# Weight blocks in halves on two DMA queues, and the second tile's statistics behind the first tile's normalising, at the head of a fused attention and FFN kernel

## Chip, cores, metric

One core of one Trainium2 chip. The metric is the device time of one execution in microseconds (us), slowest core (here the only one). The profile's span is some 1.7 to 3.5 us shorter than the time of the same run.

## The reference

```python
x  = A_x                                   # [1, 2048, 1024] bf16
xn = layernorm(x)                          # no gain, no bias
# A: 32-head linear attention
q, k, v = split(xn @ wqkv)                 # wqkv [1024, 3072]
phi = lambda t: where(t > 0, t + 1, exp(t)) + 1e-6
kv, z = phi(k).T @ v, sum(phi(k))          # per head, over all 2048 rows
s = (phi(q) @ kv / (phi(q) @ z + 1e-6)) @ wo
# B: SwiGLU
g = silu((silu(xn @ w_gate) * (xn @ w_up)) @ w_down)     # F = 3584
out = x + s * g
```

## The kernel before

The program plans itself. Every operation is put into a graph with a modelled duration; a list scheduler orders them per engine, and that order is emitted with semaphores.

Terms: a transfer is issued on SP's queue (SyncE) or ACT's (ScalarE) and lands when its last byte is there; an evacuation copies a finished product out of TensorE's result buffer `ps`; DVE is VectorE.

The head: x comes in tiles of 128 rows, the K weights in four blocks of 512 rows by 512 columns (512 KB each). I call the blocks R01 and R11 (column half j = 1, row halves k = 0 and 1; the first product needs them) and R00 and R10 (column half j = 0).

```python
def wkv_load(w, j, k):
    ap, r = kvblock(w, KB_OF[k, j])
    c0 = 1024 * (1 + w) + j * 512
    o = dma([], [r], ap, wqkv_v[:, 4 * k:4 * k + 4, c0:c0 + 512], dsem("wkv%d%d%d" % (w, j, k)), 512 * KB)
    if (w, k) == (0, 0):
        beside.append(o)                   # issued by ScalarE: R01 and R00; R11 and R10 by SP

def ln_tile(i):
    ...
    oA = dve([s.sub(0, KB).r], [sA], lambda h: h.bn_stats(stats[:, j, 0, :], xa[:, 0:512]), 512)
    oB = dve([s.sub(KB, KB).r], [sB], lambda h: h.bn_stats(stats[:, j, 1, :], xa[:, 512:1024]), 512)
    if i == 1:
        for o, q in zip((oA, oB), first):  # statistics of tile 1 wait for these two
            o.preds.add(q)
            q.succs.append(o)
    dve([sA, sB], [mvr], lambda h: h.bn_aggr(mv[:, j, :], stats[:, j, :, :]), 60)
    if i == 0:
        o0 = act([mvr, el_r], [ver], veps[:, j, :], mv[:, j, 1:2], ACT.Sqrt, "sb", bias=epsl[:, :])
        first.append(o0)
        dve([ver], [rsr], lambda h: h.reciprocal(rstd[:, j, :], veps[:, j, :]), 60)
    ...
        for c in range(0, 1024, n):        # normalise, two halves (tiles 0 and 1)
            ...
        first.append(o0)

order: x0 | x1 | R01 | R11 | R00 | R10 | x2 | V blocks ...
then:  ln_tile(0); t_tile(0); ln_tile(1); p_piece(0, 0, 1); t_tile(1); p_piece(1, 0, 1); p_piece(0, 0, 0); ...
```

`t_tile` transposes a normalised tile on TensorE (eight 128x128 blocks) and evacuates it; for tile 1 half by ScalarE, half by VectorE. `p_piece(i, 0, j)` is the product of x tile i with the K columns j, eight matmuls, evacuated by `phi_evac`: two ScalarE instructions (Exp, Relu) and two VectorE ones.

Of the kernel before, what the change touches and what calls it, by code (L numbers as in the profile page):

```python
# [14 lines left out]
KB = 1024  # L15
# [304 lines left out]
def build_kernel(nc, A_x, A_wqkv, A_wo, B_w_gate, B_w_up, B_w_down, out, WINDOW=6, NWARM=15, NPE=2, LEAD=12.0):  # L320
# [6 lines left out]
    wqkv_v = A_wqkv.rearrange("(kt p) c -> p kt c", p=128)  # L327
# [5 lines left out]
    with ExitStack() as es:  # L333
# [20 lines left out]
        def named(*key):  # L354
            return Region([key])
# [37 lines left out]
        def balloc(fresh=False):  # L393

            if fresh and bare and (len(banks) < 3 or freed[bare[0]] < freed[banks[0]]):
                b = bare.popleft()
                is_bare.discard(b)
                return b
            return banks.popleft()
# [7 lines left out]
        def bfree(b):  # L407
            freed[b] = len(PL.ops)
            (bare if b in is_bare else banks).append(b)

        def sem(name):
            return es.enter_context(nc.semaphore(name))
# [4 lines left out]
        def dsem(name):  # L417
            if name not in semn:
                semn[name] = sem("d_" + name)
            return semn[name]  # L420
# [4 lines left out]
        def mm_cost(mms):  # L425
            return sum(max(r.shape[-1] / 2400.0 + 0.0026, 0.03) * (o.shape[0] * r.shape[0] / 16384.0)
                       for (o, _, r, _, _) in mms)

        def pe_mm(reads, writes, mms):
            return PL.op("pe", reads, writes, partial(_mm_group, mms), mm_cost(mms))  # L430
# [10 lines left out]
        def act(reads, writes, o, i, func, src="ps", **kw):  # L441
            q = PL.op("act", reads, writes, lambda h: h.activation(o, i, func, **kw),  # L442
                      nel(o) / (1000.0 if "bias" in kw or not isinstance(kw.get("scale", 1.0), float) else 1200.0)
                      + (0.055 if src == "ps" else 0.095))
            if func not in (ACT.Identity, ACT.Relu):
                PL.table(q, func)
            return q

        def dve(reads, writes, fn, n, rate=0.96):
            return PL.op("dve", reads, writes, fn, n / (rate * 1000.0) + 0.07)  # L450
# [4 lines left out]
        def dma(reads, writes, o, i, s, nbytes, cow=None, after=None):  # L455
            return PL.op("sp", reads, writes, lambda h: h.dma_start(o, i), 0.47, sem=s,  # L456
                         nbytes=nbytes * (1.45 if nbytes in (128 * KB, 896 * KB) else 1.0), cow=cow,
                         after=after)
# [33 lines left out]
        def pool(reads, writes, fn, busy=0.3):  # L492
            return PL.op("pool", reads, writes, fn, busy)
# [82 lines left out]
        for n in range(NWARM):  # L576
            b = n % 8
            m = 512 if n > 3 else 128
# [154 lines left out]
        def kvblock(w, b):  # L733
            o = KV0[w] + b * 4 * KB
            return H.at(o, 4 * KB).rearrange("p (kt n) -> p kt n", n=512), H.reg(o, 4 * KB)
# [27 lines left out]
        def wkv_load(w, j, k):  # L763
            ap, r = kvblock(w, KB_OF[k, j])
            c0 = 1024 * (1 + w) + j * 512
            o = dma([], [r], ap, wqkv_v[:, 4 * k:4 * k + 4, c0:c0 + 512], dsem("wkv%d%d%d" % (w, j, k)), 512 * KB)
            if (w, k) == (0, 0):
                beside.append(o)

        xnslot = {}  # L770
        first, beside = [], []

        def ln_tile(i):
            j = i % 4
            s = xslot[i]
            xa = s.ap()
            sA, sB, mvr, ver, rsr, nmr = (named(n, j) for n in ("sA", "sB", "mv", "ve", "rs", "nm"))
# [3 lines that stand above are left out]
                for o, q in zip((oA, oB), first):  # L781
                    o.preds.add(q)
                    q.succs.append(o)
            dve([sA, sB], [mvr], lambda h: h.bn_aggr(mv[:, j, :], stats[:, j, :, :]), 60)
            if i == 0:
                o0 = act([mvr, el_r], [ver], veps[:, j, :], mv[:, j, 1:2], ACT.Sqrt, "sb", bias=epsl[:, :])
                first.append(o0)
                dve([ver], [rsr], lambda h: h.reciprocal(rstd[:, j, :], veps[:, j, :]), 60)
            else:
                o0 = dve([mvr], [ver], lambda h: h.tensor_scalar(veps[:, j, :], mv[:, j, 1:2], EPS_LN, None, ALU.add), 60)  # L790
                pool([ver, nh_r], [rsr], lambda h: h.tensor_tensor(rstd[:, j, :], veps[:, j, :], neg_half[:, :], ALU.pow), 0.56)
            o = xn_ring.take()
            xnslot[i] = o
            oa = o.ap(FP16)
            if i < 2:
                n = 512
                for c in range(0, 1024, n):
                    p0, o0 = o0, dve([s.r, mvr, rsr], [o.sub(2 * c, 2 * n).r], lambda h, c=c: h.tensor_scalar(
                        oa[:, c:c + n], xa[:, c:c + n], mv[:, j, 0:1], rstd[:, j, :], ALU.subtract, ALU.mult), n, 2.6)
                    if c:  # L800
                        o0.after = (p0,)
                        p0.succs.append(o0)
                first.append(o0)
            else:
                dve([mvr, rsr], [nmr], lambda h: h.scalar_tensor_tensor(
                    nmean[:, j, :], mv[:, j, 0:1], -1.0, rstd[:, j, :], ALU.mult, ALU.mult), 60)
                act([s.r, nmr, rsr], [o.r], oa, xa, ACT.Identity, "sb", bias=nmean[:, j, :], scale=rstd[:, j, :])

        def xt_dest(i):
            p, j, m = i // 8, (i // 4) % 2, i % 4  # L810
            ar = X if p == 0 else P
            return ar, j, m
# [26 lines left out]
        def xt_r(i, k0=0, n=KT):  # L839
            ar, j, m = xt_dest(i)  # L840
            keys = []
            for kt in range(k0, k0 + n):
                o = j * 8 * KB + kt * 1024 + m * 256
                keys += ar.reg(o, 256).keys
            return Region(keys)

        def xt_ap(i, kt):
            ar, j, m = xt_dest(i)
            return ar.at(j * 8 * KB + kt * 1024 + m * 256, 256, FP16)
# [33 lines left out]
        def k_evac(i, j, ap, r, kind):  # L883
            if i not in pkv:
                pkv[i] = pk_ring.take()
            s = pkv[i].sub(j * 1024, 1024)
            phi_evac(ap, r, s.ap(), s.r, kind, rl_rings[0])
# [4 lines left out]
        def v_evac(i, j, ap, r):  # L892
            act([r, vx_r[i % 4]], [named("vx", i % 4, j)], v_dest(i, j), ap.rearrange("p (g n) -> p g n", n=128),
                ACT.Identity)

        def p_piece(i, w, j):
            b = balloc(True)
            n = 2 if (i, w, j) == (0, 0, 1) else 4
            for k0 in range(0, KT, n):
                ap, r = KVV[w]["R%d%d" % (k0 // 4, j)]  # L900
                pe_mm([xt_r(i, k0, n), r], [bank_r[b]],
                      [(ps[b][:, :], xt_ap(i, k), ap[:, k % 4, :], k == 0, k == KT - 1) for k in range(k0, k0 + n)])
            if w == 0:
                k_evac(i, j, ps[b][:, :], bank_r[b], "ps")
            else:
                v_evac(i, j, ps[b][:, :], bank_r[b])
            bfree(b)
# [50 lines left out]
        for n, (fn, args) in enumerate(((x_load, (0,)), (x_load, (1,)), (wkv_load, (0, 1, 0)), (wkv_load, (0, 1, 1)),  # L958
# [3 lines left out]
            k = len(PL.ops)  # L962
            fn(*args)
            for o in PL.ops[k:]:
                o.urgent = 60.0 - 2 * n
        ln_tile(0)
        t_tile(0)
        tr = [o for o in PL.ops if o.eng == "pe"][-1]
        for n in range(6):
            o = pe_mm(wz_r[:1], [bank_r[kvb[2]]], [(ps[kvb[2]][:, 0:128], wz[:, 0:128], wz[:, 0:128], True, True)])  # L970
            o.preds.add(tr)
            tr.succs.append(o)
            o.urgent = -4.0
        ln_tile(1)
        p_piece(0, 0, 1)
        t_tile(1)
        p_piece(1, 0, 1)
        p_piece(0, 0, 0)
        x_load(4)
        x_load(5)  # L980
        p_piece(1, 0, 0)
        ln_tile(2)
        p_piece(0, 1, 1)
        t_tile(2)
# [60 lines left out]
        for q, kb in enumerate(kvb):  # L1045
            n = 3 if q < 2 else 2
# [777 lines left out]
```

## Time and profile before

| | before |
|---|---|
| time, median of 3 runs | 712.3 us (711.97 to 712.69) |
| profiled run | 713.57 us, span 711.8 us |
| TensorE busy | 705.0 us of the span |
| TensorE without a matmul between 5 and 10.5 us | about 0.8 us |

TensorE is the bound and has no gap from 10.51 us to far beyond; all that the change can move is the moment at which that stretch begins. The lines that show it are in the prediction.

### The profile page before, as it was taken

Reading aid. Unit: us, or ns where it says so; the run is one execution under the profiler, and the core shown is the slowest. Engines: PE = TensorE matmul, PEld = TensorE weight load, DVE = VectorE, ACT = ScalarE, POOL = GpSimd, SP = SyncE. Lnnn points to the kernel's source line nnn. Section 1 sums busy time; section 2 is a strip of 40 time slices with the busy share of each in tenths; the row PEclk is TensorE's granted clock in tenths of the full one; section 3 lists DMA queues with packets and bytes.
Section 4 is the critical chain, followed back from the end, with each engine's and each line's share of the span. In section 5 each row is a group of like instructions: output and inputs, shape, how many; then the busy total and the mean of one; then the engine's idle time right before and its main releaser. Section 6 shows DMA issues by size and latency. Waiting matters only on the chain.

```text
span 711.8 us, 11445 instructions
## 1 busy us (share of the span) xinstructions
PE 705.0 (99%) x4181; PEld 387.3 (54%) x4181; DVE 630.9 (89%) x1534; ACT 424.7 (60%) x827; POOL 12.8 (2%) x34
## 2 busy tenths in 40 slices
PE   8999999999999999999999999999999999999997
PEld 4444445555555555556555455555555555565654
DVE  6999858989999999988958989999999999797863
ACT  5788756988679566663212257876886756531212
POOL 2111000000000000000000000000000000000000
PEclk9999999999999999999999999999999999999999
DMA  9654134345664252326499955323715241646763
GB/s 310 133 99 110 30 118 123 116 143 186 187 178 141 95 171 90 119 71 175 120 233 198 215 142 149 107 73 94 207 60 192 76 149 60 184 134 168 136 160 92
DMA packets 140872, 98.66 MB, mean 139 GB/s; under 512 B 34960, under 2 KB 137872, under 8 KB 140816
## 3 DMA queue, kind: packets, MB, share of 16 engines
q1 hardware_dynamic: 139472, 96.69, 49.8%
q10 hardware_dynamic: 1344, 1.25, 0.5%
q8 instruction: 33, 0.54, 0.3%
q14 instruction: 23, 0.19, 0.1%
HBM read 77.59 MB, written 12.71 MB: 127 GB/s over the span
## 4 chain that ended last, share of the span: by engine, by line
PE 93%; DMA 3%; DVE 3%; issue 0%; SPq 0%; ACT 0%; DVEq 0%
PE ps L309 93%; DVE W L453 1%; DMA W<-in_B_w_gate_dram 1%; DMA H<-in_A_wqkv_dram 1%; DMA TM<-TM 1%; DVE TM L453 1%; DVE X L453 0%; DVE ps L453 0%; PE ps L316 0%; DVE P L453 0%; SPq L456 0%; SPq L760 0%; ACT TM L442 0%; SPq L1621 0%; DVEq L301 0%
## 5 line engine op out<-in xcount | busy, mean ns | idle before, releaser
L309 PE MATMUL ps<-X,W 128*128 128x512 f16 (+2 forms) x1372 | 288.8, 350 | 0.0
L442 ACT ACTIVATE TM<-ps 128x512 f16<-128x512 f32 (+3 forms) x386 | 202.8, 554 | 103.9 <-PE ps L309 97.8
L309 PE MATMUL ps<-H,W 128*128 128x512 f16 (+2 forms) x1096 | 218.4, 351 | 0.1
L453 DVE TENSOR_TENSOR W<-W 128x1024 f16<-128x1024 bf16 (+5 forms) x412 | 184.6, 484 | 5.0 <-PE ps L309 2.7
L309 PEld LDWEIGHTS ps<-X,W 128*128 128x128 f16 (+1 forms) x1372 | 132.1, 98 | 103.8 <-ACT H L442 1.0
L309 PEld LDWEIGHTS ps<-H,W 128*128 128x128 f16 (+1 forms) x1096 | 105.8, 98 | 95.3 <-DVE ps L453 1.1
L453 DVE TENSOR_TENSOR ps<-ps,TM 128x256 f32<-128x256 f32 (+1 forms) x250 | 132.5, 531 | 14.4 <-PE ps L309 11.2
L442 ACT ACTIVATE ps<-ps 128x512 f32<-128x512 f32 (+1 forms) x174 | 85.8, 494 | 89.9 <-PE ps L309 89.4
L442 ACT ACTIVATE H<-ps 128x512 f16<-128x512 f32 (+1 forms) x132 | 78.4, 605 | 37.9 <-PE ps L309 37.9
L309 PE MATMUL ps<-P,W 128*128 128x256 f16 (+1 forms) x516 | 99.5, 319 | 0.0
L453 DVE TENSOR_TENSOR H<-H 128x1024 f16<-128x1024 f16 (+5 forms) x126 | 71.9, 585 | 0.6 <-ACT H L442 0.4
L442 ACT ACTIVATE TM<-TM 128x512 f16<-128x512 f32 (+1 forms) x70 | 44.0, 630 | 44.5 <-DVE TM L453 43.4
L309 PEld LDWEIGHTS ps<-P,W 128*128 128x128 f16 (+1 forms) x516 | 50.1, 98 | 29.1 <-ACT TM L442 0.8
L309 PE MATMUL ps<-W 128*128 128x256 f16 (+1 forms) x330 | 62.3, 282 | 0.4 <-DVE ps L453 0.2
L453 DVE TENSOR_TENSOR H<-H,TM 128x512 f16<-128x512 f16 (+1 forms) x120 | 48.4, 420 | 8.5 <-ACT H L442 8.3
L453 DVE TENSOR_TENSOR TM<-ps,TM 128x512 f32<-128x512 f32 (+3 forms) x63 | 41.8, 663 | 12.8 <-PE ps L309 11.9
L309 PEld LDWEIGHTS ps<-W 128*128 128x128 f16 (+1 forms) x330 | 31.3, 98 | 32.6 <-DVE ps L453 1.3
L309 PE MATMUL ps<-H,X 128*128 128x512 bf16 (+1 forms) x150 | 35.2, 379 | 0.5 <-DMA H<-in_A_wqkv_dram 0.5
L453 DVE TENSOR_TENSOR TM<-TM 128x512 bf16<-128x512 f16 (+2 forms) x73 | 29.3, 414 | 7.0 <-ACT TM L442 4.3
L309 PE MATMUL ps<-H,P 128*128 128x512 bf16 (+1 forms) x110 | 26.8, 379 | 0.0
L453 DVE TENSOR_TENSOR H<-ps,TM 128x512 f16<-128x512 f32 (+1 forms) x35 | 24.2, 690 | 2.2 <-PE ps L309 1.3
L453 DVE TENSOR_TENSOR TM<-TM,W 128x512 f16<-128x512 f16 (+1 forms) x39 | 14.2, 369 | 11.4 <-ACT TM L442 11.4
(103 smaller groups left out, 398.7 us busy)
## 6 DMA issues: line engine op xcount, KB each, us to landing
W<-in_B_w_gate_dram SPq DMA_DIRECT2D x14, 1024.0 KB, 5.4
W<-in_B_w_up_dram SPq DMA_DIRECT2D x14, 1024.0 KB, 5.5
W<-in_B_w_down_dram SPq DMA_DIRECT2D x14, 896.0 KB, 6.4
H<-r_scratch SPq DMA_DIRECT2D x32, 128.0 KB, 3.8
W<-m_scratch SPq DMA_DIRECT2D x4, 1024.0 KB, 5.2
s_scratch<-TM SPq DMA_DIRECT2D x32, 128.0 KB, 2.0
TM<-in_A_x_dram SPq DMA_DIRECT2D x16, 256.0 KB, 3.5
W<-in_A_x_dram SPq DMA_DIRECT2D x15, 256.0 KB, 3.4
```

The costliest lines, as they stand in the source:

```text
L309: last = h.matmul(o, l, r, start=st, stop=sp, skip_group_check=True)
L442: q = PL.op("act", reads, writes, lambda h: h.activation(o, i, func, **kw), nel(o) / (1000.0 if "bias" in kw or not isinstance(kw.get("sca ...
L453: return dve(reads, writes, lambda h: h.tensor_tensor(o, a, b, op), nel(o), 1.92 if fast else 0.96)
```

## The change

Intent: R01 and R11 reach the chip side by side, half of each on either queue, so that the first product does not wait for R11; and tile 1's statistics no longer stand between tile 0's reciprocal and its normalising.

```diff
         def wkv_load(w, j, k):
 ...
-            o = dma([], [r], ap, wqkv_v[:, 4 * k:4 * k + 4, c0:c0 + 512], dsem("wkv%d%d%d" % (w, j, k)), 512 * KB)
-            if (w, k) == (0, 0):
-                beside.append(o)
+            if w:
+                dma([], [r], ap, wqkv_v[:, 4 * k:4 * k + 4, c0:c0 + 512], dsem("wkv%d%d%d" % (w, j, k)), 512 * KB)
+                return
+            for h in range(2):
+                n = len(r.keys) // 2
+                o = dma([], [Region(r.keys[n * h:n * h + n])], ap[:, 2 * h:2 * h + 2],
+                        wqkv_v[:, 4 * k + 2 * h:4 * k + 2 * h + 2, c0:c0 + 512], dsem("wkv%d%d%d%d" % (w, j, k, h)),
+                        256 * KB)
+                if h:
+                    beside.append(o)
 ...
                 o0 = act([mvr, el_r], [ver], veps[:, j, :], mv[:, j, 1:2], ACT.Sqrt, "sb", bias=epsl[:, :])
-                first.append(o0)
 ...
                         p0.succs.append(o0)
-                first.append(o0)
+                    first.append(o0)
 ...
                 ap, r = KVV[w]["R%d%d" % (k0 // 4, j)]
+                if n == 2:
+                    m = len(r.keys) // 2
+                    r = Region(r.keys[m * (k0 // 2 % 2):][:m])
```

## The prediction

> **What bounds the kernel now.** I read the busy table first, then the chain that ended last, then the head of the kernel in order of time, then the bytes of each DMA queue, because the diff touches only the first K weight blocks and the first two x tiles.
>
> The busy table says that TensorE is the bound:
>
> ```profile
> span 711.8 us, 11445 instructions
> PE 705.0 (99%) x4181; PEld 387.3 (54%) x4181; DVE 630.9 (89%) x1534; ACT 424.7 (60%) x827; POOL 12.8 (2%) x34
> ```
>
> Only 711.8 - 705.0 = 6.8 us of the span have no matmul. The busy table by stage places them: 1.04 us before the first matmul, about 0.8 us between 5 and 10.5 us (2.23 busy of 2.50, then 2.48 of 3.00), 1.1 us in the 600 us from 50 to 650, and 4 us at the end. So a change in the head is worth at most what it moves the point from which TensorE no longer stops. The chain, restricted to the first 40 us, shows that point:
>
> ```profile
> 1.75 7.16 DMA H<-in_A_wqkv_dram
> 8.90 0.14 issue
> 9.04 1.02 PE ps L309 x4
> 10.06 0.45 PE ps L316 x8
> 10.51 18.25 PE ps L309 x96
> ```
>
> Columns are start, duration, what. One weight block, issued on the SP queue at 1.75, lands at 8.91; four matmuls wait for it; then the eight transposes of x tile 1; from 10.51 matmuls follow each other without a gap. That block is R11, K rows 512 to 1023 of columns 512 to 1023, the second half of the first product (it is the first of the two full blocks that SP issues). Everything after is TensorE work, so the time moves by what 10.51 moves, unless something later gives it back.
>
> The timeline of the head, by engine (start, busy us, engine, line, what; in brackets the idle time before it):
>
> ```profile
> 1.04 5.30 PE L309 MATMUL ps<-TM 128*128 128x128 f16 x15 [1.04 <-DVE TM L574]
> 6.60 0.72 PE L316 MATMUL ps<-ident,W 128*128 128x128 f16 x8 [0.27 <-DVE W L798]
> 7.50 1.03 PE L309 MATMUL ps<-H,X 128*128 128x512 bf16 x4
> 9.04 1.02 PE L309 MATMUL ps<-H,X 128*128 128x512 bf16 x4 [0.52 <-DMA H<-in_A_wqkv_dram]
> 9.90 0.61 PE L316 MATMUL ps<-ident,W 128*128 128x128 f16 x8
> ...
> 5.48 0.16 DVE L788 RECIPROCAL rstd<-veps 128x1 f32<-128x1 f32 x1 [0.36 <-ACT veps L442]
> 5.56 0.67 DVE L778 BATCH_NORM_STATS2 stats<-W 128x6 f32<-128x512 bf16 x1
> 6.15 0.72 DVE L798 TENSOR_SCALAR W<-W,mv,rstd 128x512 f16<-128x512 bf16 x2
> 6.91 0.69 DVE L779 BATCH_NORM_STATS2 stats<-W 128x6 f32<-128x512 bf16 x1
> 8.71 0.73 DVE L798 TENSOR_SCALAR W<-W,mv,rstd 128x512 f16<-128x512 bf16 x2 [0.68 <-POOL rstd L791]
> ```
>
> Two things to see. The statistics of tile 1 (5.56) stand between the reciprocal of tile 0 and the normalising of tile 0 (6.15): 6.15 - 5.56 = 0.59 us on the path to the first transpose. And the warm-up matmuls keep TensorE busy to 1.04 + 5.30 = 6.34, so only 0.27 us of that shows as idle TensorE.
>
> **What the Trainium skill says.** "DMA: Bandwidth & Descriptors", section "Issuing engines are not separate DMA queues": transfers from SP and ACT run on the same 16 engines, and issuing from several saves only issue time. The trace agrees: from 5 to 6 us the ACT queue alone moves 0.37 MB of 0.38; from 8 to 9 SP alone moves 0.35. So two queues bring no bandwidth; the change can only alter which block comes first. The same page, "Queues, rings and completion order", has each engine take turns between queues. The trace agrees in part: from 6.25 to 6.5 us they move 0.05 (ACT) and 0.04 MB (SP), but from 5.0 to 5.75 SP moves nothing, though its block was issued at 1.75. "Perfetto Trace Analysis", section "DMA Instruction — HWDGE (DVE, Sync)", has the descriptor generator locked by one issuer until its descriptors are made; that would let ACT's second 512 KB block, issued 30 ns before SP's, hold SP back. No view shows the generator, so I treat this as a guess. "TensorE: Matmul & The Clock Gate", section "Back-to-back issue gap", gives about N/2.4 + 2.5 ns between warm matmuls, 216 ns for 512 columns; here four take 1.03 us with 0.38 for one alone, (1.03 - 0.38)/3 = 0.217 us. It agrees, so eight without a wait take 7 x 0.217 + 0.38 = 1.90 us.
>
> **The change, part by part.**
>
> *Statistics wait for the normalising.* Nothing is removed; one 0.67 us DVE instruction moves behind two that take 0.72 together. Normalising can start at about 5.65 (end of the reciprocal at 5.64), about 0.5 us earlier. The first transpose followed the start of normalising by 6.60 - 6.15 = 0.45, which gives 6.1; but TensorE is in its warm-up until 6.34. So transposes start at 6.35: 0.25 us earlier. The evacuations (6.93, 1.21 us for four) and the first product (7.50) follow 0.25 earlier: first matmul at 7.25, four done at 8.28, last evacuation at 7.9. Tile 1: the DVE order has the same sum, so its aggregate stays at about 7.63 and its normalising at 8.71 to 9.44. Gain of this part alone: none at 10.51, because the first product would still wait for R11 at 9.04.
>
> *Halves on two queues.* The same 2 MB in 1 KB rows, eight transfers for four. SP still carries 2 blocks' worth, ACT too. Issue time: SP and ACT each have two more issues of about 0.5 us. On ACT the square-root table load moves from 2.27 to about 3.3, ends near 4.6 (1.28 us), still before the Sqrt at 5.15; 0.55 us spare. When do the halves land? Summing the bytes of both queues second by second gives 0.23 MB by 3 us, 0.56 by 4, 0.94 by 5, 1.32 by 6, 1.69 by 7, 2.03 by 8. Before, R11 was SP's third item, up to 0.13 + 0.26 + 0.52 = 0.92 MB of that queue, reached at 8.2, while ACT had already moved all its 1.18 MB; it landed 0.7 later. After, in order of issue, up to R11's last half come x0 (0.26), x1 (0.26), four halves of R01 and R11 (1.05), and perhaps one half of the next block from ACT (0.26): 1.57 to 1.84 MB, at 6.7 to 7.4, landing at 7.4 to 8.1. R01 lies within the first 1.31 MB, at 6.0, landing by 6.7: before 7.25. The fifth matmul wants R11 at 8.28. So the 0.52 us wait goes, and the first product runs 7.25 to about 9.2 in place of 10.06.
>
> *What then binds.* The transposes of tile 1 need its normalising: first half done near 9.1, second at 9.44, and 0.25 to 0.45 us from there to TensorE (6.15 to 6.60 before). So they run about 9.25 to 9.9, against an end of 10.51. Gain there: 0.6 us. Some of it can be lost in the next group: before, the matmuls at 11.24 had waited for ScalarE's evacuation of tile 1, which itself stands behind the first exponential (10.10, 0.60 us); that chain starts 0.6 earlier too but after a 0.59 us evacuation; I take off 0.1. Net: 0.5 us at the point from which TensorE no longer stops.
>
> *Later.* VectorE is 7.47 of 8 us busy from 14 to 22 us, which could take the gain back; but at 28.0 it had waited 0.99 us for TensorE, so it has that slack. The order of instructions is planned by the program itself from modelled durations, so the new dependences can reorder work anywhere; the loss to be had or saved is small, since from 50 to 650 us only 1.1 us are idle. I allow 0.5 us either way. Sum: 712.3 - 0.5 = 711.8.
>
> **Rivals.**
> 1. *R11 lands no earlier.* SP's position of its last half is the same 0.92 MB of the queue as before (0.13 + 0.26 + two halves). If SP is starved as it was from 5 to 5.75, it lands at 8.9 again, and the time stays at 712.3. For it: that stall has no proven cause. Against it: ACT would have to run all 1.18 MB ahead again, and its transfers are now half as long.
> 2. *R01's first half comes late.* It is now on SP, behind 0.13 + 0.26 MB; at SP's old pace (0.57 MB by 7 us) its 0.66 MB would land near 7.95, after the 7.25 at which the product wants it; the first product would end near 10.1. Time 712.3 to 712.5.
> 3. *The ACT queue holds up ScalarE.* SP's later issues took up to 2.36 us when blocked. If ACT's third and fourth issue were so blocked, the table load and Sqrt, then all of tile 0, come up to 1 us late: 713. Against it: ACT had issued the same bytes by 2.23.
> 4. *The plan shifts for the worse or better elsewhere*: plus or minus 1 us.
>
> **Range and chances.** The first account has about 0.6, rivals 1 and 2 together 0.3, the third 0.1; with the plan's shifts and the spread of the three runs before (711.97 to 712.69) I put 8 in 10 on 710.9 to 712.8. Two per cent is 14.2 us; all idle time of TensorE is 6.8. Faster by over 2% is impossible by this route; slower would need a broken plan.
>
> **What would show it.** Right: no statistics between reciprocal and normalising; first transpose at 6.3 to 6.4; first product's eight matmuls without a DMA wait, from 7.2 to 9.3; tile 1's transposes over by 9.9; the long piece of TensorE in the chain starting near 9.9. Wrong: a DMA wait before the first or fifth matmul (rivals 1, 2), Sqrt later than 5.2 (rival 3), more than 1.5 us idle on TensorE from 50 to 650 (rival 4).

## The result, and the profile after

Ratios are the mean time of one kernel's fast runs over that of the other's in the same rounds, so they are not quite the ratio of the medians quoted beside them. The changed kernel took 712.46 us (median of 6, 712.02 to 713.88) against 712.31 of before (6 runs): ratio 1.0007, 95% interval 0.9994 to 1.002. In a second set it was 711.93 against 712.29: 0.9994 (0.9982 to 1.0006). So the runs resolve no difference. The second interval alone would still allow the 0.5 us that I forecast; that it did not come is read from the marks within the traces, below.

The profiled span, on the other hand, is 709.9 us against 711.8. That is the first thing to explain away. The busy table of TensorE by stretch (start:end, us, busy us, matmuls, clock, DMA share, GB/s), before:

```profile
400.00:408.00 8.00, 7.76 (x43) 1.00 0.76 187
408.00:417.00 9.00, 8.21 (x46) 1.00 0.97 163
```

after:

```profile
400.00:408.00 8.00, 8.00 (x45) 1.00 0.67 173
408.00:417.00 9.00, 9.00 (x50) 1.00 0.69 187
```

In the trace of before TensorE stood still for 1.03 us here, 400 us away from the change, and the matmuls that follow ran 1.6 us earlier in the trace of after. The timeline of TensorE in the trace of before shows where:

```profile
407.62 0.39 PE L309 MATMUL ps<-W 128*128 128x256 f16 x2 [0.24 <-DVE ps L453]
...
416.46 0.39 PE L309 MATMUL ps<-W,TM 128*128 128x256 f16 x2 [0.62 <-DVE ps L453]
```

Ahead of the second stop VectorE in turn had waited 1.52 us for a w_gate block that took 8.1 us from issue to landing there and 5.7 in the trace after. Of the 14 traces, only this one has that stall; the other 13, three of them of the same kernel, are busy for 20.00 of the 20 us from 400 to 420. So it does not belong to the kernel and says nothing about the change.

Now the head. The chain that ended last, first 40 us, after:

```profile
2.19 6.26 DMA H<-in_A_wqkv_dram
8.44 0.14 issue
8.58 1.04 PE ps L309 x4
...
9.64 1.08 ACT TM L442 x2
10.72 0.50 ACT X L442
...
11.27 28.86 PE ps L309 x144
```

The wait for R11 is still there (0.33 us in place of 0.52) and ends 0.46 us earlier: four matmuls start at 8.58 in place of 9.04. But a link has joined the chain that was not in it: ScalarE, with two evacuations of the first product and then tile 1's, and the stretch without a gap begins at 11.27. TensorE's timeline after:

```profile
6.33 0.72 PE L316 MATMUL ps<-ident,W 128*128 128x128 f16 x8 [0.67 <-DVE W L804]
...
7.22 1.03 PE L309 MATMUL ps<-H,X 128*128 128x512 bf16 x4
8.58 1.02 PE L309 MATMUL ps<-H,X 128*128 128x512 bf16 x4 [0.33 <-DMA H<-in_A_wqkv_dram]
9.44 0.66 PE L316 MATMUL ps<-ident,W 128*128 128x128 f16 x8
10.08 1.02 PE L309 MATMUL ps<-H,X 128*128 128x512 bf16 x4
11.27 2.98 PE L309 MATMUL ps<-H,X 128*128 128x512 bf16 x13 [0.16 <-ACT X L442]
```

The last line is the new wait. ScalarE's timeline shows why. Before:

```profile
10.10 0.60 ACT L442 ACTIVATE TM<-ps 128x512 f16<-128x512 f32 x1 [0.66 <-PE ps L309]
10.59 0.59 ACT L442 ACTIVATE X<-ps 128x512 f16<-128x512 f16 x1
11.07 0.60 ACT L442 ACTIVATE TM<-ps 128x512 f16<-128x512 f32 x1
```

After:

```profile
9.64 1.08 ACT L442 ACTIVATE TM<-ps 128x512 f16<-128x512 f32 x2 [0.47 <-PE ps L309]
10.61 0.60 ACT L442 ACTIVATE X<-ps 128x512 f16<-128x512 f16 x1
```

TM<-ps are the Exp and the Relu of the first product; X<-ps is tile 1's transposed half, which the next matmuls need. Before, the order was Exp, tile 1, Relu. After, it is Exp, Relu, tile 1. Nothing in the diff asks for that; the plan did it. Its modelled start times, printed from the program itself:

```
            Exp     tile 1   Relu
before      9.96    10.44    10.93
after       9.50    10.46     9.98
```

In the model the first product ends earlier, tile 1's transposes do not, and Relu fits into the hole between (9.98 to 10.46). On the chip there is no hole: the transposes come right behind the product.

To compare traces whose DMA timing differs I use two marks on TensorE: the start of the fifth matmul of the first product (the end of the wait for R11), and a landmark further on, eight transposes of a block in H near 125 us, with no idle TensorE between about 12 us and there. Before and after:

```profile
124.67 0.61 PE L316 MATMUL ps<-ident,H 128*128 128x128 f16 x8
```

```profile
124.65 0.61 PE L316 MATMUL ps<-ident,H 128*128 128x128 f16 x8
```

So of 9.04 - 8.58 = 0.46 us gained at the fifth matmul, 0.02 are left at the landmark. From mark to mark it is 124.67 - 9.04 = 115.63 us before and 124.65 - 8.58 = 116.07 after: 0.44 lost.

### The profile page after: what moved, and what is told of

Read it like the earlier page. It is cut to its first block, busy times and chain, and to the rows that moved or that the text cites. A ratio compares the mean times of both kernels' runs of the same rounds, so it can differ in the third digit from the quotient of the medians.

```text
span 709.9 us, 11452 instructions
## 1 busy us (share of the span) xinstructions
PE 704.1 (99%) x4181; PEld 387.9 (55%) x4181; DVE 631.1 (89%) x1534; ACT 425.3 (60%) x827; POOL 13.3 (2%) x34
## 4 chain that ended last, share of the span: by engine, by line
PE 98%; DMA 1%; ACT 0%; SPq 0%; issue 0%; DVE 0%
PE ps L309 98%; DMA H<-in_A_wqkv_dram 1%; ACT TM L442 0%; PE ps L316 0%; SPq L456 0%; ACT X L442 0%; DVE TM L453 0%; SPq L760 0%
```

## The experiments

Theory: the halves bring R11 earlier, and the statistics part, by way of the plan, takes the same amount back on ScalarE. Rivals: the gain in the span is real and belongs to the kernel (the stall); the halves bring nothing; the loss comes from other reorderings (the plan also moved some matmuls on TensorE).

### The two kernels again

No edit, to see what a trace repeats.

> The kernel before, unchanged: a control for the trace. Theory (the gain in the head is taken back there; the 1.9 us between the two profiled spans is a stall near 407 to 417 us that comes and goes in both kernels): head as before, the wait for R11 ending at 9.04 plus or minus 0.1, the eight transposes of x tile 8 at 124.67 plus or minus 0.1, time within 0.1% of before; among its runs both spans near 710 and spans near 712. Rival (the stall belongs to the kernel before, the changed one is rid of it): its span is 711.5 or more in nearly every run, and the stall is in this profile too.

> The changed kernel, unchanged. Theory: matmuls on tile 1 start again at 11.27 plus or minus 0.1 behind ScalarE's evacuation, landmark at 124.65 plus or minus 0.1; statistics of tile 0 start again near 3.77 only if the later landing of x tile 0 (3.58 before) belongs to the change, near 3.6 if it was chance. Spans of its runs between 709.7 and 712.1. Time within 0.1% of before.

Times: 712.36 against 712.29 (ratio 1.0004, 0.9987 to 1.002) and 711.93 against 712.29 (0.9994). Spans of single runs: before 709.6 to 712.4, the changed kernel 709.7 to 712.1. The stall near 410 us is in neither. So both kernels have runs near 710 and near 712, and the rival that gives the changed kernel a better span falls.

The expectation for the marks was wrong in one way and useful in another. TensorE in the second trace of before:

```profile
8.26 1.03 PE L309 MATMUL ps<-H,X 128*128 128x512 bf16 x4
9.77 1.02 PE L309 MATMUL ps<-H,X 128*128 128x512 bf16 x4 [0.48 <-DMA H<-in_A_wqkv_dram]
...
125.40 0.61 PE L316 MATMUL ps<-ident,H 128*128 128x128 f16 x8
```

R11 came 0.73 us later than in the first trace of the same kernel (I had allowed 0.1), so the landing times at the head scatter by more than the whole effect that I look for. But 125.40 - 9.77 = 115.63, to the hundredth what it was; and in the second trace of the changed kernel 125.18 - 9.11 = 116.07, again to the hundredth. The distance between the marks is the instrument. The later landing of x0 (3.77) did not repeat (3.46): chance.

### Each part alone

Halves only: the diff's first and last hunks, with the statistics as before. In this kernel the plan keeps the order of before on TensorE and ScalarE.

```diff
+                first.append(o0)          # after the Sqrt, as before
-                    first.append(o0)
+                first.append(o0)          # once behind the loop, as before
```

> Halves on two queues, statistics as before; its order of instructions is that of the kernel before on TensorE and ScalarE. Theory (halves bring 0.4 us, the statistics part takes it back by putting the second evacuation of the first product ahead of tile 1's on ScalarE): wait for R11 ends at 8.6, transposes of tile 1 at 9.4, tile 1 evacuated by 10.75, matmuls go on at 10.95 without a wait for ScalarE, landmark 124.25 to 124.35. Rival (the halves themselves bring nothing, since tile 1's normalising or ScalarE binds anyway): landmark at 124.6 to 124.7. Time 711.9 by the theory against 712.3.

Statistics only: the opposite.

```diff
                 o0 = act([mvr, el_r], [ver], veps[:, j, :], mv[:, j, 1:2], ACT.Sqrt, "sb", bias=epsl[:, :])
-                first.append(o0)
 ...
-                first.append(o0)
+                    first.append(o0)
```

> Only the statistics part, whole blocks on one queue each. Theory: the wait for R11 ends at 9.04 as before, transposes of tile 1 over at 10.5, ScalarE then runs its two product evacuations (10.1 to 11.1) before tile 1's (11.07 to 11.67), so matmuls on tile 1 start at 11.7 against 11.24: landmark 125.0, about 0.35 us slower. Rival (earlier normalising is worth something by itself): landmark at 124.67 or below.

Halves only: 712.58 against 712.29 (1.0001, 0.9989 to 1.0013). TensorE:

```profile
9.22 1.02 PE L309 MATMUL ps<-H,X 128*128 128x512 bf16 x4 [0.49 <-DMA H<-in_A_wqkv_dram]
10.08 0.61 PE L316 MATMUL ps<-ident,W 128*128 128x128 f16 x8
10.73 3.61 PE L309 MATMUL ps<-H,X 128*128 128x512 bf16 x16
```

No wait for ScalarE, as the theory says. But R11 came at 9.22, not 8.6, so the landmark was at 125.01 and the stated 124.25 to 124.35 missed. From mark to mark it is 125.01 - 9.22 = 115.79, so 0.16 more than before: the four matmuls behind tile 1's transposes start 0.65 us after these (10.08 to 10.73) where it was 0.45 before (9.90 to 10.35). They need R00. In halves its first half is the fifth transfer of SP's queue (the expectation of a later run calls it fourth, by counting badly). Issued at 2.70, it landed 7.9 us later, at 10.59, 0.14 before those matmuls; in all six traces in halves it landed 1.50 to 1.52 us behind R11's last half, which is why the 0.16 repeats. Before, R00 was third on ACT's queue and landed at 8.24.

Statistics only: 712.82 against 712.29 (1.0006, 0.9992 to 1.0019). TensorE:

```profile
9.43 1.02 PE L309 MATMUL ps<-H,X 128*128 128x512 bf16 x4 [1.17 <-DMA H<-in_A_wqkv_dram]
...
12.12 2.12 PE L309 MATMUL ps<-H,X 128*128 128x512 bf16 x9 [0.36 <-ACT X L442]
```

The landmark was at 125.50 and not at the 125.0 expected, since R11 was late again; but 125.50 - 9.43 = 116.07: with whole blocks and this part alone the 0.44 us are there in full. The earlier normalising brought the first four matmuls to 7.23, and then the product waited 1.17 us for R11: worth nothing while R11 binds. The rival for this run falls.

### ScalarE's order alone, both ways

One ScalarE instruction is moved after planning; TensorE's order stays. In the changed kernel Relu goes behind tile 1's evacuation:

```diff
         PL.schedule()
+        mv_, at_ = marks["relu"], marks[1]     # Relu of the first product; tile 1's evacuation
+        PL.order.remove(mv_)
+        PL.order.insert(PL.order.index(at_) + 1, mv_)
```

> The changed kernel with one ScalarE instruction moved after planning: the second evacuation of the first product goes behind tile 1's evacuation, as in the kernel before. Measure: from the start of the fifth matmul (end of the wait for R11) to the landmark (the eight transposes near 125 us), which was 115.63 in both traces of before, 116.07 in both of the changed kernel and in stats_only, 115.79 in halves_only. Theory (ScalarE's order is the loss): 115.75 to 115.8, and matmuls on tile 1 go on without a wait for ScalarE over 0.2. Rival (the loss comes from the other reorderings of TensorE that the plan made): 116.07 still.

In the kernel before it goes ahead of it:

```diff
         PL.schedule()
+        mv_, at_ = marks["relu"], marks[1]
+        PL.order.remove(mv_)
+        PL.order.insert(PL.order.index(at_), mv_)
```

> The kernel before with the same ScalarE instruction moved ahead of tile 1's evacuation, nothing else. Theory: fifth matmul to landmark 116.07 in place of 115.63, with a wait for ScalarE of 0.3 to 0.4 on TensorE. Rival: 115.63.

The changed kernel with the order put right:

```profile
8.70 1.02 PE L309 MATMUL ps<-H,X 128*128 128x512 bf16 x4 [0.42 <-DMA H<-in_A_wqkv_dram]
...
10.21 4.05 PE L309 MATMUL ps<-H,X 128*128 128x512 bf16 x18
```

There is no wait for ScalarE; the landmark is at 124.48, difference 115.78, as expected by the theory. The kernel before with the order spoilt: fifth matmul 8.76, then

```profile
11.45 2.76 PE L309 MATMUL ps<-H,X 128*128 128x512 bf16 x12 [0.36 <-ACT X L442]
```

and the landmark at 124.89, difference 116.13 (expected 116.07). So this one instruction's place makes the wait for ScalarE appear and go, and with it 0.50 us in the kernel before (115.63 to 116.13) and 0.29 in the changed kernel (116.07 to 115.78). The rest of the 0.44 there is R00's lateness, which halves_only has too (115.79) and which the wait for ScalarE had hidden. The plan's other reorderings, present in the first and absent in the second, cost nothing that the marks show. In time neither can be told from before: 1.0003 (0.9990 to 1.0015) and 1.0000 (0.9987 to 1.0013). Tenths of a microsecond are below what five rounds resolve.

### Only the first product's blocks in halves

R00 whole on ACT's queue again, to keep its place; once with the statistics as before, once with the statistics part and ScalarE's order put right.

```diff
-            if w:
-                dma([], [r], ap, ..., 512 * KB)
+            if w or j == 0:
+                o = dma([], [r], ap, ..., 512 * KB)
+                if (w, k) == (0, 0):
+                    beside.append(o)
                 return
```

> Statistics as before; only the two blocks of the first product come in halves, the next (R00) whole on ACT's queue as before. Theory (halves bring R11 0.44 earlier, but put R00's first half fourth on SP, 0.16 to 0.2 lost behind it): fifth matmul at 8.6 to 9.2, then to the landmark 115.63, no gap between the transposes of tile 1 and the next four matmuls; about 0.4 us faster than before, 711.9. Rival (R11 early only because R00 was late): R11 no earlier than 9.2 to 9.4.

> As split_j1 with the statistics part of the change as well and ScalarE's order put right. Theory: R11 still binds, so the same as split_j1: fifth matmul at 8.6 to 9.2, then 115.63 to the landmark; 711.9. If R11 is early enough not to bind, the earlier normalising shows for once: fifth matmul at 8.3 to 8.5. Rival (reorderings elsewhere cost): more than 115.75 to the landmark.

The first took 713.25 against 711.94 (ratio 1.0012, 0.9999 to 1.0025), the second 711.67 (0.9991, 0.9978 to 1.0005): neither a gain that can be told. TensorE in the first:

```profile
7.66 1.89 PE L309 MATMUL ps<-H,X 128*128 128x512 bf16 x8
9.38 0.68 PE L316 MATMUL ps<-ident,W 128*128 128x128 f16 x8
10.35 3.84 PE L309 MATMUL ps<-H,X 128*128 128x512 bf16 x17 [0.29 <-DMA H<-in_A_wqkv_dram]
```

All eight matmuls of the product run without a wait here, as the prediction wanted; and the wait has gone to R00, which landed at 10.31. In the second kernel the product still waited 0.47 us for R11 (fifth matmul 8.75), and the matmuls behind tile 1's transposes 0.49 us for R00, landed at 10.66. The landmarks, 124.65 and 124.96, are no better than before, and from mark to mark it is 116.13 and 116.21 where I expected 115.63. My expectation (no gap behind tile 1's transposes) failed in both: R00's place on ACT's queue, with the same bytes ahead of it there as before, was not what kept it early. In the trace of split_j1 the blocks came in the order of need and the last of them was late.

### Two more looks at each

> The kernel before, for one more trace of R11's landing, since single traces scatter (fifth matmul at 9.04, 9.77, 9.43, 8.76 with whole blocks, mean 9.25; 8.58, 9.11, 9.22, 8.70 with four blocks in halves, mean 8.90). Theory (halves bring R11 about 0.4 us earlier on the mean): between 8.8 and 9.8. Rival (halves bring nothing, the difference was chance): the four new looks of the two kinds mix, or turn round. From the fifth matmul to the landmark 115.63 either way.

> The changed kernel with ScalarE's order put right, for one more trace. Theory: fifth matmul between 8.5 and 9.2; R00 late again, so four matmuls later by about 0.2 after tile 1's transposes, and 115.78 from the fifth matmul to the landmark. Rival: fifth matmul at 9.2 or later.

> As whole_look1: fifth matmul between 8.8 and 9.8 by the theory, mean of all six with whole blocks near 9.25; 115.63 to the landmark.

> As halves_look1: fifth matmul between 8.5 and 9.2 by the theory, mean of all six in halves near 8.9; 115.78 to the landmark.

Single runs of 712.00, 712.41, 711.43 and 711.29 us. All the traces together:

| trace | K blocks | ScalarE before tile 1 | fifth matmul | landmark | difference |
|---|---|---|---|---|---|
| before | whole | Exp | 9.04 | 124.67 | 115.63 |
| before_again | whole | Exp | 9.77 | 125.40 | 115.63 |
| whole_look1 | whole | Exp | 8.95 | 124.88 | 115.93 (0.17 wait for R00) |
| whole_look2 | whole | Exp | 8.84 * | 124.55 | 115.71 (R00 just late) |
| stats_only | whole | Exp, Relu | 9.43 | 125.50 | 116.07 |
| before_relu_first | whole | Exp, Relu | 8.76 | 124.89 | 116.13 |
| after | halves | Exp, Relu | 8.58 | 124.65 | 116.07 |
| after_again | halves | Exp, Relu | 9.11 | 125.18 | 116.07 |
| halves_only | halves | Exp | 9.22 | 125.01 | 115.79 |
| after_x_first | halves | Exp | 8.70 | 124.48 | 115.78 |
| halves_look1 | halves | Exp | 8.82 | 124.62 | 115.80 |
| halves_look2 | halves | Exp | 8.64 | 124.42 | 115.78 |
| split_j1 | R01, R11 in halves | Exp | 8.52 * | 124.65 | 116.13 (0.29 wait for R00) |
| split_j1_stats_x_first | R01, R11 in halves | Exp | 8.75 | 124.96 | 116.21 (0.49 wait for R00) |

(* Shown there as one piece of eight matmuls; 8.84 and 8.52 are the start of tile 1's transposes, 9.70 and 9.38, less the 0.86 us that lie between the two in the other traces.)

The difference obeys the theory, and its misses all lie with R00. They are the two kernels with only R01 and R11 in halves and, of the kernel before, whole_look1 and whole_look2, which should have been 115.63: R00 landed at 10.54 and 10.21 there, just ahead of the matmuls that need it (10.59 and 10.26). With whole blocks it landed anywhere from 8.24 to 10.54. The fifth matmul has mean 9.13 with whole blocks and 8.85 with four blocks in halves, six traces each, so 0.29 us earlier; with a scatter of 0.4 and 0.3 within the kinds the error of that is about 0.2. The four new looks alone differ by less (8.90 and 8.73); with the two split_j1 kernels counted the halves have 8.79. That the halves bring R11 earlier is likely and not shown; the two kinds overlap (8.76 to 9.77, and 8.58 to 9.22).

## Why the prediction was wrong

Point by point, in its own steps.

- **The bound, and what of it can move.** Right: nothing beyond the head was moved, and 2% was never in reach.
- **Statistics behind the normalising.** The order on VectorE is as foreseen and the first transposes started at 6.33 (predicted 6.35), the first product at 7.22 (7.25). The agreement is partly luck: x0 landed 0.19 us later in that trace, and the warm-up ended at 5.66 rather than 6.34. That this part alone gains nothing was right, and too kind: by itself it loses 0.44 us.
- **R11's landing.** Failed in size. The text has it "landing at 7.4 to 8.1", and concludes that the first product runs without a wait from 7.25. It landed at 8.45 in that trace and between 8.45 and 9.09 in six, so 0.33 to 0.49 us of wait stay. R11's two halves did not come side by side: ACT's landed at 7.32 to 7.79, about as foreseen, and SP's 0.69 to 1.30 us later. I counted the bytes ahead of it (1.57 to 1.84 MB) with the byte clock of one trace of before. In two traces (after, after_x_first) the queues had moved 1.81 and 1.86 MB by 0.7 us before R11's landing, about the count, but that was at 7.75 and 7.87 us and not by 7.4: from 3 to 4 us they moved 205 and 190 GB/s where the trace of before had moved 322 (second trace of before: 188). In two others (after_again, halves_only) it was 2.16 and 2.11 MB, so more had gone ahead than the one half block that I allowed. The gain at the fifth matmul was put at 9.04 - 8.28 = 0.76 us and is 0.29, with an error of 0.2.
- **What then binds.** Here the step failed that decided the sign. For ScalarE's evacuation of tile 1 the prediction said "I take off 0.1". It costs 0.44 (against the two traces of before in which R00 was early), because the plan placed Relu ahead of it; between the fifth matmul and the first weight load on tile 1 lie 2.20 us with the old order (before) and 2.69 with the new (stats_only). I saw that chain in the profile and assumed its order fixed, although I wrote that "the new dependences can reorder work anywhere" and sized such a shift from the middle of the kernel, where TensorE stands idle for 1.1 us in 600, not from the head, where it waits for single instructions.
- **R00.** Not foreseen as a cost: in halves it landed at 9.94 to 10.59 and held the matmuls behind tile 1's transposes, 0.16 us from mark to mark. In the changed kernel it is hidden behind the wait for ScalarE.
- **Rivals.** Rival 1 (R11 no earlier) is half true. Rival 2 did not happen in the trace after (R01's SP half landed at 6.62). In three of the six traces in halves that half landed at 7.24 to 7.58 and held the first matmul until 7.37 to 7.71, short of the rival's 7.95 and hidden behind the wait for R11. Rival 3 did not happen: ScalarE's four issues took 2.01 us; the Sqrt ran at 5.33, past the 5.2 named as a sign, because tile 0's statistics ended late (5.30). Rival 4 did, in the head; its sign, idle time from 50 to 650, did not show (0.06 us).
- **A small misreading.** ACT's second block was issued 40 ns before SP's, not 30; nothing but a guess rested on it.

The sum with measured terms: -0.29 at the fifth matmul, +0.44 behind it, together +0.15 with an error of 0.2 (against the mean of all four traces of before, 115.73, the second term is +0.34 and the sum +0.05). The measured times, 712.46 against 712.31 and 711.93 against 712.29, are compatible with that and with zero; they cannot tell more.

Open: how much the halves bring on R11, and why the queues share the engines so differently from run to run. None of the versions tried beats the kernel before by an amount that the runs resolve.

## What to carry to other kernels

In a kernel that plans itself, a new dependence changes orders that the diff doesn't show: compare the instruction order of each engine before and after, and look first at the engine that hands work to the bound one. Where landing times scatter more than the effect, do not compare times or spans but the distance between two marks inside one trace, which here repeated to a few hundredths of a microsecond as long as no other landing (R00's) came between the marks. And when transfers are limited by bandwidth, a block that comes earlier makes another one later: ask which, and who waits for it.

## What the Trainium skill lacked or had wrong

- "DMA: Bandwidth & Descriptors", "Queues, rings and completion order": engines take turns between the queues. It lacks that the share differs between executions: with the same program R11 landed at 8.91 and 9.64 us, and from 5 to 6 us ACT moved 0.37 and 0.30 MB against 0.01 and 0.06 of SP. Its statement in "Issuing engines are not separate DMA queues" (no bandwidth from a second queue) agrees with the two traces compared: halves on two queues moved 348 to 369 GB/s in each microsecond from 6 to 9 (trace after), whole blocks 348 to 362 (trace before).
- The same page, "Specifications", gives a limit of about 358 GB/s for HBM to one core. The row lacks the condition that the page has under "Bandwidth", that both cores of a pair are streaming. The trace of before, of a program on one core, moved 384 GB/s in each of the two microseconds from 4 to 6, later about 350.
- "TensorE: Matmul & The Clock Gate", "Back-to-back issue gap", has 131 ns per matmul of 512 columns in a stream with weight loads, and 216 ns as the isolated gap. Here the stream of weight loads and matmuls shows the latter: eight in 1.89 us with 0.38 for one, (1.89 - 0.38)/7 = 0.216 us.
- No page says that the profile of one execution can hold a stall that the next does not: 1.03 us of TensorE near 407 to 417 us in one trace of 14, behind which its matmuls ran 1.6 us later than those of the changed kernel, most of the 1.9 us between the two spans.
